# A planned attention and state-space kernel: the prologue laid out anew

## The chip, the cores and the metric

The kernel runs on one core of one Trainium2 chip. The engines named below are TensorE (PE, with its weight loads as PEld), VectorE (DVE), ScalarE (ACT), GpSimd (POOL) and SyncE (SP, which here only issues transfers). The metric is the device time of one execution in microseconds (us). The kernel before takes 701.06 us, the median of three runs between 700.88 and 701.33.

## What is computed

Two results on 2,048 rows of 640 columns stand side by side in the output. The first is a state-space layer on `A_x`, the second is attention with 32 query heads of 20 columns that share one key head and one value head, on `B_x`:

```python
h = Lam_bar[None, :] * h + Bu[:, t, :]              # A: a scan over t, 640 complex states
y = 2.0 * einsum("blp,dp->bld", hseq, Cmat).real + x * Dskip
q = (x @ wq) -> 32 heads of 20; k = x @ wk; v = x @ wv     # B
p = softmax(q k^T * 20 ** -0.5); o = p @ v; out_B = o @ wo
```

Inputs and output are bf16. The attention needs 32 x 2,048 x 2,048 exponentials, 134 million, and this is most of the work.

## The kernel before, in words

**Tiles.** The scores are made as 2,048 blocks of 128 keys x 512 queries. Of a block's 512 queries all belong to one head. Keys and queries have 20 columns plus a row that carries a bound, so a block uses a 32-row strip of the PE array, and three or four blocks run side by side in one *fill* (a matmul in four 32-row strips). A fill goes into a slot of three banks of PSUM, SC0 or SC1. Two or three of its blocks get their exp on ACT (one ACTIVATE over 1,024 or 1,536 columns, line 1519, into PR); the third block of a fill with two is turned by DVE into an approximate exponential (line 864: a scaled conversion to int16, whose bits are read as bf16), to which POOL (line 1834) and DVE add constants for four shifted variants whose products with differently scaled values (VS) are added up. The products with the values (PR with VP, BIG with VS, line 727) run on PE in four 32-column strips and collect in the bank MB3. The last free bank, MB2, and the third banks of the slots serve all the other work: query projections, the state-space part, the output projection.

**The bound.** In place of a maximum over scores, each query's row gets a bound: the absolute query times a matrix that holds the largest absolute key of each column, times a negative constant. `mab` holds the key maxima, `mask0` the constant in the shape of the matrix, M0 their product. M0 times the absolute queries is added to the queries' own PSUM bank; the result, lifted by a constant, is evicted to QT.

**The prologue** does this, in front of the first exp: x of the first two blocks of 512 rows (tb 0 and 1) is loaded as it is (`xn`, into the buffer CT) and turned by PE against a unit matrix, with evictions by ACT and DVE into xbT (lines 1132 and 1135); x of blocks 2 and 3 (`XB`) comes by transposing transfers. Keys of the four blocks are made on PE (line 1155) from wks, four copies of wk beside each other (line 1040, on ACT). After each block's keys DVE takes the maximum over its columns (line 1161) and DVE or ACT evicts the keys to KT (lines 864 and 1167). The first queries (`qt_task`, g = 0) come from wqp (line 1272), are evicted by ACT (line 1285), and wait for M0. DVE takes the maximum of the five partial maxima (line 1187) and makes M0 (line 863). PE adds the product, DVE evicts to QT (line 864), the first fill follows. The last block's keys are made in halves (`KEY_STEPS`), with a reduction for each. Values (`v_task`, line 1211) are made for the blocks 0 and 1 in banks of SC1 in between. Meanwhile the vectors of the state-space part (`vrow`: log_dt, Lambda_re, Lambda_im, Dskip) feed a chain of small steps for its tables.

**The queues.** SP issues Lambda_re, the two plain x loads, Dskip, the first 80 columns of wq, the transposing loads of x, wv, the rest of wq, then the B matrices. ACT's queue issues log_dt, Lambda_im and wk. POOL makes masks, the integer steps of the angle tables, wqp, and fills VS and QT with zeros.

**What sets the order.** The program is not written in the order in which it runs. `Schedule` plays the whole kernel through with durations given for each step: each engine takes, whenever it is free, the ready step of the lowest `prio`, subject to gates (`gate`), to slack that keeps urgent steps free, and to parameters that change with the number of blocks done (`STAGES`). Transfers of the prologue have assumed landing times (`LANDS` and the last column of `XB`). A seed (`SEEDS`) varies it. The order that results is emitted engine by engine, with semaphore waits. So a changed step in the prologue, or another seed, gives another order of everything behind it too.

```python
fill = self.pe([], self.mmt(512, 2), deps=deps, prio=0, mode="S", hook=lambda op, i=i: self.fill(op, i))
```

This is a fill in `attention()`: its deps are the last exps of the slot, the queries of its block, and the keys.

Of the kernel before, what the change touches and what calls it, by code (L numbers as in the profile page):

```python
# [11 lines left out]
ACT = mybir.ActivationFunctionType  # L12
# [454 lines left out]
class Build:  # L467
# [77 lines left out]
    SEEDS, REPLAYS = (10005,), 12  # L545
# [418 lines left out]
    def constants(self):  # L964
# [12 lines left out]
        def fill(t, v, dur):  # L977
            return "dve", lambda e: e.memset(t, v), dur
# [31 lines left out]
        many("VS", [("pool", lambda e: e.memset(p.VS[:], 0.0), 1850)] + [fill(p.VS[:, k, :, 20:21], c, 100) for k, (_, c) in enumerate(self.SHIFTS)])  # L1010
# [12 lines left out]
    def loads(self):  # L1023
# [7 lines left out]
                                       eng=eng, writes=[f"vrow{i}"], prio=0) for i, v in enumerate((self.log_dt, self.Lre, self.Lim, self.Dskip))]  # L1031
        self.vec_op = [vec[0]("act"), vec[1]("sp"), vec[2]("act")]
# [15 lines left out]
        self.vec_op.append(vec[3]("sp"))  # L1048
# [72 lines left out]
    def kv_steps(self):  # L1121
# [20 lines left out]
        def kv(tb):  # L1142
            yield lambda: all((tb, c) in self.xb_op for c in range(NC)) and (tb < self.PLAIN or self.s.done([self.xb_op[tb, 0]])) \
                and any(x in self.early for x in self.free_banks)
            bank = self.take(self.early, self.KEY_BANKS)
            prev = None
            steps = [(0, c, 512) for c in range(NC)] if tb < 3 else self.KEY_STEPS
            for x, c, n in steps:
                at = 512 * tb + n * x
# [4 lines left out]
                else:  # L1154
# [3 lines left out]
                                   self.mmt(n), prio=self.KP[tb], deps=[self.xb_op[tb, c], self.wks_op] + bank.last, prev=prev,  # L1158
                                   mode="F", load=float(n), reads=[f"xbT{tb}_{c}", "wks"], writes=[bank.key])
                if c == NC - 1:  # L1160
                    red = self.dve(lambda e, src=bank.cols(n * x, n * x + n), to=p.mab[:, tb + x:tb + x + 1]: e.tensor_reduce(  # L1161
                        out=to, in_=src, axis=AX.X, op=ALU.max, apply_absolute_value=True), 115 + 1.05 * n, deps=[prev], reads=[bank.key],
                        writes=[f"mab{tb + x}"], prio=0.31 if tb < 3 or x else 0.315)
                    self.red_op[tb + x] = red
            dst, src = p.KT[:, 512 * tb:512 * tb + 512], bank.ap
            if self.KEYS[tb] == "a":
                kt = self.act(lambda e: e.activation(dst, src, ACT.Identity, bias=p.lift[:, 2:3], scale=ALPHA * UNIT), 600,
                              deps=[red, self.lift_op], reads=[bank.key, "lift"], writes=[f"KT{tb}"], prio=0.34)
            else:
                kt = self.dve(self.ts(dst, src, ALPHA * UNIT, p.lift[:, 2:3], ALU.mult, ALU.add), 640,  # L1170
                              deps=[red, self.lift_op], reads=[bank.key, "lift"], writes=[f"KT{tb}"], prio=0.44)
# [4 lines left out]
            if tb < 2:  # L1176
                yield lambda: any(x in self.early for x in self.free_banks)
                yield from self.v_task(tb, self.take(self.early, self.KEY_BANKS))
            else:
                self.tasks.append((self.V_AT[tb - 2], 0, lambda: self.started, lambda bank: self.v_task(tb, bank)))  # L1180
                self.tasks.sort(key=lambda t: t[0])

        self.red_op = {}

        def bound():
            yield lambda: len(self.red_op) == 5
            m = self.dve(lambda e: e.tensor_reduce(out=p.mab[:, 5:6], in_=p.mab[:, 0:5], axis=AX.X, op=ALU.max), 120,
                         deps=list(self.red_op.values()), reads=[f"mab{i}" for i in range(5)], writes=["mabs"], prio=0.3)
# [1427 lines left out]
```

## Time and profile before

| | |
|---|---|
| median of three runs | 701.06 us |
| the profiled execution | 701.27 us, with a span of 699.5 us |
| busy in the span | PE 684.9, ACT 685.4, DVE 630.2, POOL 467.7 us |
| exps on ACT | 677, of which 566 of two blocks and 111 of three |
| granted PE clock | 0.999 of full |

The span runs from the first instruction of the program to the last; the device time has some 1.8 us more around it. In rows of groups, the columns are line, engine, operation, what is written and read (the buffers' numbers are left out, so SC is SC0 or SC1, M is M0), shapes, count; then busy time in us, the mean duration of one in ns; then the idle time of the engine in front of them and what ended it. In rows in order of time the first two numbers are start and duration in us, and what stands in brackets is the idle time ahead and its releaser. A PE row such as `32*128 32x512` is a weight of 32 x 128 against 512 columns. In rows of stretches there is the length, the busy time with the count, the granted clock, the share of the transfer engines and GB/s. Consecutive instructions of an engine overlap a little, so the mean duration of one is longer than its share of the busy time.

### The profile page before, as it was taken

To read this page: it belongs to the slowest core of one execution; us is meant where nothing else is said; L and a number is where in the kernel's file an instruction comes from. 1 tells how busy PE (TensorE), PEld (TensorE's weight loads), DVE (VectorE), ACT (ScalarE), POOL (GpSimd) and SP (SyncE) were. 2 spreads that over 40 slices of the span, in tenths; PEclk is the share of its full clock that TensorE was granted. 3 is DMA by queue.
4 is the path that set the end of the run, shared out by engine and by line. 5 is a ranking of instruction groups with operands and counts; after the bars stand their busy time and mean duration, and the time that the engine had idled before them with its cause. 6 is when DMAs were issued, how large, how long until landed. Compare 5 with 4: busy or idle time off the path is not lost.

```text
span 699.5 us, 27013 instructions
## 1 busy us (share of the span) xinstructions
PE 684.9 (98%) x11350; PEld 248.1 (35%) x11350; DVE 630.2 (90%) x1211; ACT 685.4 (98%) x701; POOL 467.7 (67%) x796
## 2 busy tenths in 40 slices
PE   9999999999999999999999999999999999999997
PEld 5323232334323333534343323334333333343323
DVE  7899899999999988898979997899999999997695
ACT  7999999999999999999999999999999999999996
POOL 4266776443868898464777885767866777768780
PEclk9999999999999999999999999999999999999999
DMA  9649831101111111000030010120000011100101
GB/s 220 174 107 211 184 89 58 28 8 31 28 48 32 28 43 37 22 19 16 17 83 20 15 42 21 36 55 22 12 15 20 12 26 39 32 20 15 27 15 40
DMA packets 77590, 34.46 MB, mean 49 GB/s; under 512 B 58350, under 2 KB 77470, under 8 KB 77470
## 3 DMA queue, kind: packets, MB, share of 16 engines
q1 hardware_dynamic: 76506, 32.44, 19.3%
q8 instruction: 91, 1.49, 0.9%
q10 hardware_dynamic: 964, 0.29, 0.2%
q14 instruction: 29, 0.24, 0.1%
HBM read 11.53 MB, written 9.75 MB: 30 GB/s over the span
## 4 chain that ended last, share of the span: by engine, by line
PE 66%; ACT 33%; DVE 0%; issue 0%; DVEq 0%
ACT PR L1519 33%; PE MB L727 26%; PE MB L797 17%; PE SC L727 14%; PE MB L807 7%; PE SC L1155 1%; PE MB L723 1%; PE SC L723 0%; DVE PR L859 0%; PE MB L1272 0%; DVE mab L1161 0%; DVEq L510 0%; PE SC L1211 0%; DVE pvsb L859 0%; DVE M L863 0%
## 5 line engine op out<-in xcount | busy, mean ns | idle before, releaser
L1519 ACT ACTIVATE PR<-SC 128x1024 bf16<-128x1024 f32 (+1 forms) x677 | 670.5, 1177 | 4.0 <-PE SC L727 2.9
L1834 POOL INT64_ADD BIG<-BIG x761 | 455.4, 614 | 200.8 <-DVE BIG L864 71.8
L864 DVE TENSOR_SCALAR BIG<-SC 128x512 int16<-128x512 f32 x548 | 369.1, 684 | 48.9 <-PE SC L727 42.6
L727 PE MATMUL SC<-QT,KT 32*128 32x512 bf16 x2013 | 264.5, 384 | 7.0 <-ACT PR L1519 6.0
L727 PE MATMUL MB<-BIG,VS 128*32 128x512 bf16 x2332 | 257.4, 383 | 0.4 <-DVE pvsb L1901 0.2
L727 PE MATMUL MB<-PR,VP 128*32 128x512 bf16 x1465 | 213.7, 384 | 0.0
L727 PEld LDWEIGHTS SC<-QT,KT 32*128 32x128 bf16 x2013 | 66.6, 91 | 157.4 <-ACT PR L1519 94.5
L727 PEld LDWEIGHTS MB<-BIG,VS 128*32 128x32 bf16 x2332 | 61.6, 95 | 65.1 <-issue 40.2
L727 PEld LDWEIGHTS MB<-PR,VP 128*32 128x32 bf16 x1465 | 51.4, 94 | 44.6 <-issue 32.5
L797 PE MATMUL MB<-CT,W 128*32 128x320 bf16 (+2 forms) x996 | 52.6, 301 | 0.6 <-issue 0.6
L864 DVE TENSOR_SCALAR BIG<-BIG 128x1024 int16<-128x1024 int16 (+1 forms) x116 | 45.8, 427 | 1.7 <-PE MB L727 1.3
L807 PE MATMUL MB<-xaT,BT 32*128 32x256 bf16 x200 | 38.6, 272 | 0.7 <-ACT PR L1519 0.6
L797 PE MATMUL MB<-CA,W 128*32 128x512 bf16 (+1 forms) x640 | 35.5, 302 | 0.0
L797 PE MATMUL MB<-xaT,BA 128*32 128x256 bf16 x800 | 32.2, 275 | 0.0
L807 PE MATMUL MB<-diagD,xaT 32*128 32x128 bf16 x320 | 31.4, 217 | 0.0
L807 PEld LDWEIGHTS MB<-diagD,xaT 32*128 32x128 bf16 x320 | 17.7, 92 | 28.9 <-ACT PR L1519 19.3
L797 PEld LDWEIGHTS MB<-CT,W 128*32 128x32 bf16 x996 | 22.4, 96 | 15.2 <-issue 7.5
L2086 DVE CAST stg<-MB 128x512 bf16<-128x512 f32 x35 | 23.9, 682 | 2.5 <-PE MB L797 2.5
L797 PE MATMUL MB<-xaT,BT 128*32 128x256 bf16 x600 | 25.1, 274 | 0.0
L859 DVE TENSOR_TENSOR prod<-MB,tab 128x1024 bf16<-128x1024 f32 x20 | 24.3, 1217 | 0.4 <-PE MB L797 0.2
L864 DVE TENSOR_SCALAR BIG<-MB 128x512 int16<-128x512 f32 x35 | 23.8, 679 | 0.0
L2353 DVE TENSOR_TENSOR_SCAN g<-sc,hst,prod 128x256 bf16<-128x256 f32 x30 | 22.9, 774 | 0.1
(174 smaller groups left out, 488.3 us busy)
## 6 DMA issues: line engine op xcount, KB each, us to landing
out_dram<-stg SPq DMA_DIRECT2D x31, 128.0 KB, 1.8
qd<-BIG SPq DMA_DIRECT2D x20, 128.0 KB, 2.4
QT<-qd SPq DMA_DIRECT2D x28, 80.0 KB
OP<-pvsb SPq DMA_DIRECT2D x105, 20.0 KB
rdP<-recs SPq DMA_DIRECT2D x105, 20.0 KB
lbd<-BA SPq DMA_DIRECT2D x5, 320.0 KB, 4.0
CT<-in_B_x_dram SPq DMA_DIRECT2D x2, 640.0 KB, 5.3
BA<-in_A_B_re_dram SPq DMA_DIRECT2D x1, 800.0 KB, 7.0
```

The costliest lines, as they stand in the source:

```text
L723: r = e.matmul(out[32 * j:32 * j + 32], lhsT=lhsT[:, 32 * j:32 * j + 32], rhs=rhs, start=start, stop=stop, tile_position=(0, 32 * j), skip ...
L727: return lambda e: e.matmul(out, lhsT=lhsT, rhs=rhs, start=start, stop=stop, **kw)
L797: x = e.matmul(out[32 * j:32 * j + 32], lhsT=lhsT[:, 32 * j:32 * j + 32], rhs=rhs, start=start, stop=r.end is tag, tile_position=(0, 32 * ...
L807: return lambda e: e.matmul(out, lhsT=lhsT[at], rhs=rhs[at], start=False, stop=r.end is tag, tile_position=(32 * row, 0), skip_group_check ...
L859: return lambda e: e.tensor_tensor(out, a, b, op)
L864: return lambda e: e.tensor_scalar(out, a, s1, s2, op0=op0, op1=op1)
L1155: prev = self.pe([lambda e, x=x, c=c, n=n, at=at: e.matmul(bank.cols(n * x, n * x + n), lhsT=p.wks[:, 128 * c:128 * c + 128], rhs=p.xbT[:, ...
L1519: ex = self.act(lambda e: e.activation(dst, t[:, 0:512 * n], ACT.Exp, scale=1.0 / UNIT), 0.8333 * 512 * n + 64, table="exp", deps=[op], re ...
L1834: op.fns.append(lambda e: e.int64_add(words(dst), words(src), add))
L2086: ev = self.dve(lambda e: e.tensor_copy(st, bank.ap), 645, deps=[prev], reads=[bank.key], writes=[key], prio=self.EV, gate=(lambda: last.e ...
L2353: o = self.dve(lambda e, ri=ri, init=init: e.tensor_tensor_scan(p.g[:, u, ri, :], rdec, p.prod[:, 1, 0, ri, :], init, ALU.mult, ALU.add), ...
```

## The change

The diff does these things.

1. **Queues.** Lambda_re and Dskip move from SP's queue to ACT's, so SP begins with the x loads. The transposing loads of the last x block are cut into pieces of 2, 2 and 1 columns of 128 instead of 3 and 2. The assumed landing times change.
2. **wks** is made by DVE, not ACT (`WKE`); the four small fills of VS go from DVE to POOL.
3. **Keys.** Each block has its own bank (`KEY_BANKS`), the last block is made whole and not in halves; its eviction and that of the third block go to DVE and ACT at later times (`KEYS`, gates).
4. **The bound in steps.** M0 is made from the maximum over three blocks by ACT (line 1188 of the new program), and when the fourth block's maximum is there DVE takes the smaller of that and mask0 times the fourth maximum (line 1192; the constant is negative). The maximum over all four, for the later blocks' bound, follows behind.
5. **First queries in two banks.** The first query block stands half in MB2 and half in a bank of SC1; ACT and DVE evict a half each, before and after the product with M0.
6. **Values** of blocks 0 and 1 are made together, in the free half of MB2, ahead of the product with M0.
7. **The first exp** waits for the first slot's two banks and the keys of the first block, and not for all banks and all keys.
8. **The plan**: another seed, other parameters in some stages, `LAST` 8 instead of 16, `CB_FROM` 341.944 instead of 358.689. With it the whole order is another one: 561 exps of two blocks and 116 of three.

```diff
-    SEEDS, REPLAYS = (10005,), 12
+    SEEDS, REPLAYS = (120680,), 12
...
-        self.vec_op = [vec[0]("act"), vec[1]("sp"), vec[2]("act")]
+        self.vec_op = [vec[0]("act"), vec[1]("act"), vec[2]("act")]
...
-        self.vec_op.append(vec[3]("sp"))
+        self.vec_op.append(vec[3]("act"))
...
-    PLAIN, KP, QR, FRP, SINP, SKIP_P, KEY_BANKS = 2, (1.04, 1.04, 1.06, 1.08), 1.05, 0.34, 0.32, 1.03, "2543016"
-    WKP, QUAD_KEYS, WKE = 0.9, 0, "a"
-    TURNED, KEYS = ("adada", "adada"), "adaa"
-    XB = ((2, 0, 5, 11250.0), (3, 0, 3, 12500.0), (3, 3, 5, 13400.0))
-    LANDS = (2250.0, 2400.0, 2750.0, 8200.0, 5600.0, 7900.0, 6500.0, 8450.0, 14600.0, 17000.0)
+    PLAIN, KP, QR, FRP, SINP, SKIP_P, KEY_BANKS = 2, (1.04, 1.04, 1.06, 1.0), 1.05, 0.34, 0.32, 1.03, ("5", "01", "3", "2")
+    WKP, QUAD_KEYS, WKE = 0.1, 0, "d"
+    TURNED, KEYS = ("adada", "adada"), "adad"
+    XB = ((2, 0, 5, 10850.0), (3, 0, 2, 12050.0), (3, 2, 4, 13270.0), (3, 4, 5, 13900.0))
+    LANDS = (2250.0, 2500.0, 2750.0, 7800.0, 5200.0, 7450.0, 6300.0, 7900.0, 14400.0, 16700.0)
...
         def bound():
-            yield lambda: len(self.red_op) == 5
-            m = self.dve(lambda e: e.tensor_reduce(out=p.mab[:, 5:6], in_=p.mab[:, 0:5], axis=AX.X, op=ALU.max), 120,
...
-            self.m0_op = self.dve(self.ts(p.M0[:], p.mask0[:], p.mab[:, 5:6], None, ALU.mult), 200, port=True,
...
+            yield lambda: all(i in self.red_op for i in range(3))
+            m = self.dve(lambda e: e.tensor_reduce(out=p.mab[:, 4:5], in_=p.mab[:, 0:3], axis=AX.X, op=ALU.max), 120,
...
+            self.m0a_op = m = self.act(lambda e: e.activation(p.M0[:].rearrange("p a b -> p (a b)"), p.mask0[:].rearrange("p a b -> p (a b)"), ACT.Copy,
+                                                scale=p.mab[:, 4:5]), 220,
...
+            yield lambda: 3 in self.red_op
+            self.m0_op = self.dve(lambda e: e.scalar_tensor_tensor(out=p.M0[:], in0=p.mask0[:], scalar=p.mab[:, 3:4], in1=p.M0[:],
+                                                                   op0=ALU.mult, op1=ALU.min), 250, port=True,
...
-    KEY_STEPS = ((0, 0, 512), (0, 1, 512), (0, 2, 512), (0, 3, 256), (0, 4, 256), (1, 3, 256), (1, 4, 256))
...
+        halves = [(bank, 0, 512, key)] if g else [(bank, 0, 256, key), (more, 256, 512, key + "b")]
...
+        if g == 0:
+            yield from self.v_task((0, 1), bank, 256, evs)
         yield lambda: self.m0_op is not None
...
-        mine = [b for _, bs in self.slots for b in bs]
-        yield lambda: all(not b.busy for b in mine)
+        yield lambda: all(not b.busy for b in self.slots[0][1][:-1])
...
-            deps += [self.kt_op[tb] for tb in range(4)]
+            deps += [self.kt_op[tb] for tb in range(min(4, (self.tile_n + 12) // 16 + 1))]
...
-    LAST = 16
+    LAST = 8
...
-    CB_FROM, CB_STEP = 358.689, 15.665
+    CB_FROM, CB_STEP = 341.944, 15.665
```

More of the change, by code (lines that the diff above doesn't have):

```diff
@@ L1405, in attention @@
             i = k % len(self.slots)
+            if k == i and k:
+                bs = self.slots[i][1][:-1]
+                yield lambda: all(not b.busy for b in bs)
+                self.slot_last[i] = [op for b in bs for op in b.last]
             yield lambda: (fill is None or fill.start is not None) and all(o.start is not None
```

178 lines of the change are left out of this document (109 added, 69 removed).

## The prediction

> **What bounds the kernel now.** I read the page first (busy time, chain), then the groups of ACT by form, then the busy time of ACT by stretch, then the first 19 us in order of time. From the page of the kernel before:
>
> ```profile
> span 699.5 us, 27013 instructions
> ...
> PE 684.9 (98%) x11350; PEld 248.1 (35%) x11350; DVE 630.2 (90%) x1211; ACT 685.4 (98%) x701; POOL 467.7 (67%) x796
> ...
> PE 66%; ACT 33%; DVE 0%; issue 0%; DVEq 0%
> ...
> L1519 ACT ACTIVATE PR<-SC 128x1024 bf16<-128x1024 f32 (+1 forms) x677 | 670.5, 1177 | 4.0 <-PE SC L727 2.9
> ```
>
> PE and ACT are both 98% busy, and the chain changes between them. The last row tells which paces: the 677 exps occupy ACT for 670.5 us, and ACT is idle only 4.0 us in front of them. So the time is three pieces: the prologue up to the first exp, the exps nearly back to back, and the tail. The groups of ACT by form, whole span, and then the same view for two neighbouring stretches of 39 us (536:575 and 575:614):
>
> ```profile
> L1519 ACT ACTIVATE PR<-SC 128x1024 bf16<-128x1024 f32 x566 | 532.9, 1106 | 4.0 <-PE SC L727 2.9 <-PE MB L727 0.7
> L1519 ACT ACTIVATE PR<-SC 128x1536 bf16<-128x1536 f32 x111 | 160.2, 1538 | 0.0
> ...
> L1519 ACT ACTIVATE PR<-SC 128x1024 bf16<-128x1024 f32 x38 | 35.9, 1076 | 0.2
> L1519 ACT ACTIVATE PR<-SC 128x1536 bf16<-128x1536 f32 x4 | 6.0, 1502 | 0.0
> ...
> L1519 ACT ACTIVATE PR<-SC 128x1024 bf16<-128x1024 f32 x38 | 36.0, 1081 | 0.9 <-PE SC L727 0.6 <-PE MB L727 0.2
> L1519 ACT ACTIVATE PR<-SC 128x1536 bf16<-128x1536 f32 x3 | 4.5, 1503 | 0.0
> ```
>
> A third block in an exp costs 1538 - 1106 = 432 ns. The stretch from 575 does one such exp fewer in the same 39 us. Busy time of the exps by stretch:
>
> ```profile
> 500.00:575.00 75.00, 74.64 (x78) 1.00 0.07 18
> 575.00:654.00 79.00, 77.47 (x82) 1.00 0.11 27
> ```
>
> ACT misses 0.36 us of 75 and then 1.53 us of 79: from 575 to 654 PE is late with its fills, elsewhere hardly. That is the one place behind the prologue where something is to be had. The prologue in order of time, one view for each engine: SP, ACT, PE's loads and PE, DVE:
>
> ```profile
> 0.81 0.39 SPq L708 DMA_DIRECT2D vrow<-in_A_Lambda_re_dram  x1
> 1.26 0.97 SPq L708 DMA_DIRECT2D CT<-in_B_x_dram  x2
> 2.27 0.49 SPq L708 DMA_DIRECT2D vrow<-in_A_Dskip_dram  x1
> ```
>
> ```profile
> 7.30 0.73 ACT L1040 ACTIVATE wks<-wkr 128x640 bf16<-128x640 bf16 x1
> ...
> 14.88 1.82 ACT L1167 ACTIVATE KT<-SC,lift 128x512 bf16<-128x512 f32 x3
> 18.16 1.02 ACT L1519 ACTIVATE PR<-SC 128x1024 bf16<-128x1024 f32 x1 [1.45 <-PE SC L727]
> ```
>
> ```profile
> 14.36 0.34 PEld L1155 LDWEIGHTS SC<-BIG,wks 128*128 128x128 bf16 x4 [0.31 <-DMA BIG<-in_B_x_dram]
> ...
> 15.05 0.66 PE L1211 MATMUL SC<-wvr,BIG 128*128 128x20 bf16 x20
> 15.57 0.59 PE L727 MATMUL MB<-PR 128*128 128x512 bf16 x2
> 16.35 0.40 PE L727 MATMUL MB<-BIG,M 128*32 128x512 bf16 x4 [0.19 <-DVE M L863]
> ...
> 17.73 0.48 PE L727 MATMUL SC<-QT,KT 32*128 32x512 bf16 x4
> ```
>
> ```profile
> 13.94 0.69 DVE L1161 TENSOR_REDUCE mab<-SC 128x1 f32<-128x512 f32 x1
> 14.55 0.28 DVE L863 TENSOR_SCALAR BIG<-QT 128x512 int16<-128x512 int16 x1
> 15.03 0.76 DVE L1161 TENSOR_REDUCE mab<-SC 128x1 f32<-128x256 f32 x2 [0.19 <-PE SC L1155]
> 15.82 0.16 DVE L1187 TENSOR_REDUCE mab<-mab 128x1 f32<-128x5 f32 x1
> 16.01 0.29 DVE L863 TENSOR_SCALAR M<-mask,mab 128x128 bf16<-128x128 f32 x1
> 16.81 0.81 DVE L864 TENSOR_SCALAR QT<-MB,lift 128x512 bf16<-128x512 f32 x1 [0.51 <-PE MB L727]
> ```
>
> The chain behind the last piece of x is to be seen: PE waits for the transfer until 14.36, two half reductions (to 15.79), their maximum, the bound's matrix M0 (to 16.30), its product with the queries (to 16.75), the last eviction of QT (to 17.62), the first fill, and the exp at 18.16. The exp idles 1.45 us for it.
>
> **The change, part by part.**
>
> *x first in its queue.* The x loads begin at 0.81 where Lambda_re stood, 0.45 us earlier; Dskip (0.49 us) no longer stands between x and the transposes. I take 0.45 for everything that lands behind them: the last piece of x at 13.9 instead of 14.36, wvr at 14.6 instead of 15.05. The transposes of the last block are cut 2, 2, 1 instead of 3, 2, so only one matmul is left behind the last landing. The three vector loads and the load of wk now stand one behind the other on ACT, whose queue grows by two issues (0.39 + 0.49) ahead of its first table load. I count nothing, since ACT's first work waits for a column that DVE makes from these very vectors; without that cover it would be those 0.9 us at most. The Trainium skill ("DMA: Bandwidth & Descriptors", Issuing engines are not separate DMA queues) says that loads of different issuing engines interleave on the same 16 engines, so that only issue time is saved. By that rule the gain is the 0.45 us of issue and no bandwidth; no row here separates the two.
>
> *wks on DVE instead of ACT.* ACT loses 0.73 us, DVE gets a copy of 640 columns between its table steps and its evictions of x. Nearest rows: 0.28 us for 512 16-bit columns on DVE, 0.73 us for this very copy on ACT. I take 0.35, as DVE's own row is nearer in kind; at 0.73 DVE's evictions, and all that hangs on them, come 0.4 us later. The Trainium skill ("VectorE: DVE Perf Modes", What auto-detection actually checks) gives a 16-bit copy within SBUF four elements a cycle, from which I estimate 0.33 us; a copy that missed the mode would take 0.82 by it, and the first exp would come 0.4 to 0.5 us later. The 0.28 us row agrees with the fast mode.
>
> *Maximum in steps, queries in two banks.* Behind the last landing: one matmul to 14.3, one reduction over 512 columns (0.69) to 15.05, one step on M0 (0.29 to 0.35) to 15.4. The maximum over the first three blocks and M0's first form (on ACT) now lie ahead of it, beside the wait for x. But PE now has all 40 value matmuls of blocks 0 and 1 queued in front of the product with M0, behind the landing of wvr: 20 hold PE from 15.05 to 15.57, so 40 take 1.05, from 14.6 to 15.65. So the product starts at 15.65, not 15.45. It is 0.40 as before (two halves of the columns), to 16.05. The eviction is split: DVE takes half the columns, 0.81 - 0.31 = 0.50 (a reduction of half the columns is 0.76 / 2 = 0.38, 0.31 below the whole one), and ACT takes the other half beside it (below the 0.6 that a KT eviction of 512 columns takes). With 0.06 from product to eviction as before, to 16.6; fill and exp follow as before (17.62 to 18.16, 0.54): first exp at 17.15. Gain 1.0 us. Ends: 1.5 if PE's queue is not late and the vectors' removal gives more; 0.45 if DVE is 0.4 late and wvr lands late. On ACT the two KT evictions (0.6 each) stand ahead of the half of QT; they start once the three-block maximum is there (about 14.4) and end at 15.7, 0.3 ahead of their successor's input; later than that by more they would set the first exp.
>
> *First exp waits for fewer keys.* It needs block 0's keys only; the third and fourth evictions go to DVE or behind. Third-bank matmuls of the next query task now wait for KT of block 3 on DVE, one eviction behind the first QT: PE has two exps at 532.9 / 566 = 0.94 us until the third needs its fill. Cost nothing, 0.3 at most.
>
> *The order that is planned anew.* It is the larger part: 561 exps of two blocks and 116 of three, so ACT gets 5 blocks more, at 0.432: +2.16 us. DVE makes 5 conversions fewer and some 24 double additions fewer, POOL 18 more; with DVE at 90% and POOL at 67% I count nothing for that. On PE the number of fills stays 677, and the streams differ by some 7 passes of 512 columns of 2,400, with five changes of mode more: nothing. But they stand elsewhere. Between exps 561 and 640, the stretch 575:654, PE has about 271 passes instead of 284, with as many three-block exps (7): 13 at 0.59 - 0.40 = 0.2 us each (two passes against one in PE's rows) are 2.6 us of room. What ACT lost there is the 1.53 idle plus some slower exps: the stretch did one exp of three blocks fewer than its neighbour in 39 us (1.4 us) and lost 0.6 idle more in its second half; I take 2.1 off. Ends: 0 (the stall moves) and 3. The remaining idle of ACT behind the first exp is 4.0 - 1.45 - 1.53 = 1.0; I halve it, -0.5, since PE gets fewer passes in the tight stretches. Behind the last exp four passes of PE stand instead of one: three at 0.2 are 0.6 at most, nothing where they run beside it; I take +0.1.
>
> Sum: -1.0 + 2.16 - 2.1 - 0.5 + 0.1 = -1.34 us: a span of 698.2. The profiled run took 701.27 us, 1.77 more than its span and 0.21 more than the median of 701.06; so 699.7 us as a median. About 0.2% (1.4 us) is what a measurement of this kernel can tell from no change, and the sum lies just at it.
>
> **Rivals.**
>
> *PE paces.* 66% of the chain speaks for it. Then the five blocks on ACT cost nothing, since ACT only fills its own gaps, and the loosened stretch and the earlier start count in full: -1.0 - 2.1 - 0.1 = about -3: 698.0. Against it: ACT idles only 4.0 us.
>
> *The prologue doesn't get faster.* PE runs in order, and wvr's landing, wk's and wq's stand closer to the work that wants them; DVE has wks in addition. If they eat the 1.0 us, the rest stays: 700.7.
>
> *Slower.* ACT paces, pays 2.16 for its blocks, and the late fills are not gone but moved: the new order was never run under these DMA times, and a stretch like 575:614 (1.3) comes up somewhere in addition. -1.0 + 2.16 + 1.3 + 0.1 = +2.56: 703.6. It decides from 0.2 us more idle than today, where the sum reaches +1.4. For it: nearly every stretch has ACT within half a per cent of full, so each added block shows. Against it: the stretch that is late today has measurably fewer passes.
>
> **How the numbers follow.** Forecast 0.50 at 699.7, its own range 698.8 to 700.6 by the prologue's ends, half of it on either side of -0.2%; PE paces 0.19 (faster); prologue not faster 0.13 (same); slower 0.18. So faster 0.24 + 0.19 = 0.43, same 0.26 + 0.13 = 0.39, slower 0.18. The range takes in the rivals' times but the outer half of each: 697.8 to 702.9.
>
> **What would show it.** The first x load at 0.81, PE's last wait for x ending near 13.9, the value matmuls running up to the product with M0, the first exp at 17.2 (a start above 17.7 says that DVE or wvr was late). The groups of ACT: 116 exps of 1536 at 1.5 us, idle ahead of the exps down from 4.0 to about 2, none of it as dense as 1.53 in 79 us. The prediction is wrong if that idle grows, if the exps take other than 2 us more in all, or if the piece behind the last exp changes by over half a us.

## The result, and the profile after

The changed kernel takes 706.19 us, the median of eight runs between 703.50 and 708.68; the kernel before, run between them, 701.29 (700.88 to 703.32). The ratio is 1.0064, with a 95% interval of 1.0042 to 1.0086: slower, where 699.7 was forecast. The profiled execution of the changed kernel is its quickest one: 703.50 us, with a span of 701.7. From its page, its groups of ACT by form, and the busy time of ACT in the two stretches shown of before and one further ahead:

```profile
span 701.7 us, 26947 instructions
...
PE 683.8 (97%) x11300; PEld 246.9 (35%) x11300; DVE 618.5 (88%) x1178; ACT 685.8 (98%) x701; POOL 478.0 (68%) x818
...
PE 52%; ACT 45%; DVE 2%; DMA 1%; issue 0%; ACTq 0%; DVEq 0%
```

```profile
L1566 ACT ACTIVATE PR<-SC 128x1024 bf16<-128x1024 f32 x561 | 528.2, 1115 | 2.0 <-PE SC L727 1.4 <-PE MB L727 0.2
L1566 ACT ACTIVATE PR<-SC 128x1536 bf16<-128x1536 f32 x116 | 168.2, 1546 | 0.5 <-PE MB L727 0.4
```

```profile
500.00:575.00 75.00, 74.86 (x78) 1.00 0.06 15
575.00:654.00 79.00, 78.50 (x83) 1.00 0.11 30
450.00:500.00 50.00, 49.06 (x52) 1.00 0.20 36
```

Much of what was forecast behind the prologue came: 116 exps of three blocks, idle time ahead of the exps down from 4.0 to 2.5 us, and the stretch from 575 misses 0.50 us instead of 1.53. Most of what was won there stands elsewhere now: between 450 and 500 ACT misses 0.94 us, where the kernel before misses 0.19. DMA has entered the chain with 1%. The start shows why; PE in order of time, first of the kernel before, then of the changed one:

```profile
4.11 0.19 PE L727 MATMUL MB<-ident,vrow 15*128 15x15 bf16 x1
4.23 2.31 PE L727 MATMUL MB<-PR 128*128 128x256 f32 x7
6.38 1.28 PE L727 MATMUL SC<-ident,CT 128*128 128x128 bf16 x20
```

```profile
6.15 0.18 PE L727 MATMUL MB<-ident,vrow 15*128 15x15 bf16 x1 [1.97 <-DMA vrow<-in_A_Lambda_im_dram]
6.25 1.56 PE L727 MATMUL MB<-PR 128*128 128x256 f32 x6
7.65 1.28 PE L727 MATMUL SC<-ident,CT 128*128 128x128 bf16 x20
...
14.28 2.32 PE L1155 MATMUL SC<-BIG,wks 128*128 128x512 bf16 x10
16.43 1.16 PE L1218 MATMUL MB<-wvr,BIG 128*128 128x20 bf16 x40
17.84 0.29 PE L727 MATMUL MB<-BIG,M 128*32 128x256 bf16 x4 [0.24 <-DVE M L1192]
...
18.99 0.40 PE L727 MATMUL SC<-QT,KT 32*128 32x512 bf16 x4
```

The small product of the vectors (MB from ident and vrow) had not waited for a transfer before. Now it waits 1.97 us for Lambda_im. Behind it, in PE's order, stand filler matmuls (MB from PR, which only keep PE busy) and the turning of x (SC from ident and CT). So x, which lands 0.5 us earlier than before (5.13 instead of 5.60, by the trace's landing of the first load), is turned 1.3 us later, and the first exp starts at 19.41 instead of 18.16. The queue of ACT, and the piece of the chain that follows from it:

```profile
0.81 0.57 ACTq L708 DMA_DIRECT2D vrow<-in_A_log_dt_dram  x1
1.42 0.27 ACTq L708 DMA_DIRECT2D vrow<-in_A_Lambda_re_dram  x1
1.72 0.32 ACTq L708 DMA_DIRECT2D vrow<-in_A_Lambda_im_dram  x1
2.08 0.41 ACTq L707 DMA_DIRECT2D wkr<-in_B_wk_dram  x1
2.52 1.02 ACTq L708 DMA_DIRECT2D vrow<-in_A_Dskip_dram  x1
```

```profile
1.72 4.38 DMA vrow<-in_A_Lambda_im_dram
```

1.2 KB are 4.38 us under way. Ahead of them two loads of x of 640 KB each were issued on the other queue, at 0.81 and 1.32. In the kernel before Lambda_im was issued at 1.40, just behind x's first load at 1.26, and was there at 2.71. The runs below test whether this place in time is the cause.

The time between the two profiled runs, in four pieces read from the exps in order of time (the 41st exp is a point behind which the prologue no longer shows):

| | before | changed | difference |
|---|---|---|---|
| first exp starts | 18.16 | 19.41 | +1.26 |
| from there to the 41st exp | 37.62 | 38.33 | +0.71 |
| 41st exp to the end of the last | 635.45 | 634.97 | -0.48 |
| behind the last exp | 8.30 | 8.94 | +0.64 |

That is +2.1 of span. The median is 2.7 above that profiled run; the runs below show where a part of that arises.

### The profile page after: what moved, and what is told of

It is laid out like the page before. It is cut to its first block, busy times and chain, and to the rows that moved or that the text cites. A ratio compares the mean times of both kernels' runs of the same rounds, so it can differ in the third digit from the quotient of the medians.

```text
span 701.7 us, 26947 instructions
## 1 busy us (share of the span) xinstructions
PE 683.8 (97%) x11300; PEld 246.9 (35%) x11300; DVE 618.5 (88%) x1178; ACT 685.8 (98%) x701; POOL 478.0 (68%) x818
## 4 chain that ended last, share of the span: by engine, by line
PE 52%; ACT 45%; DVE 2%; DMA 1%; issue 0%; ACTq 0%; DVEq 0%
ACT PR L1566 44%; PE MB L727 20%; PE MB L797 13%; PE SC L727 10%; PE MB L807 7%; DVE BIG L864 1%; PE SC L1155 1%; DMA vrow<-in_A_Lambda_im_dram 1%; PE MB L723 1%; PE SC L723 0%; DVE PR L859 0%; ACT L2199 0%; DVE pvsb L1950 0%; ACTq L708 0%; DVE mab L1161 0%
## 5 line engine op out<-in xcount | busy, mean ns | idle before, releaser
L1566 ACT ACTIVATE PR<-SC 128x1024 bf16<-128x1024 f32 (+1 forms) x677 | 671.5, 1189 | 2.5 <-PE SC L727 1.4
L1883 POOL INT64_ADD BIG<-BIG x779 | 465.0, 613 | 191.8 <-DVE BIG L864 68.9
L864 DVE TENSOR_SCALAR BIG<-SC 128x512 int16<-128x512 f32 x541 | 364.5, 684 | 62.1 <-PE SC L727 55.8
L727 PE MATMUL MB<-BIG,VS 128*32 128x512 bf16 x2312 | 265.4, 383 | 0.7 <-POOL BIG L1883 0.3
L727 PE MATMUL MB<-PR,VP 128*32 128x512 bf16 x1470 | 221.7, 384 | 0.2 <-ACT PR L1566 0.2
L727 PEld LDWEIGHTS MB<-BIG,VS 128*32 128x32 bf16 x2312 | 64.5, 95 | 65.6 <-issue 38.0
L727 PEld LDWEIGHTS MB<-PR,VP 128*32 128x32 bf16 x1470 | 53.7, 94 | 44.4 <-issue 30.2
L864 DVE TENSOR_SCALAR BIG<-BIG 128x1024 int16<-128x1024 int16 (+1 forms) x90 | 34.3, 422 | 2.4 <-PE MB L727 1.3
L807 PE MATMUL MB<-xaT,BT 32*128 32x256 bf16 x168 | 32.5, 272 | 0.3 <-ACT PR L1566 0.2
L807 PEld LDWEIGHTS MB<-diagD,xaT 32*128 32x128 bf16 x320 | 17.7, 92 | 29.0 <-ACT PR L1566 19.5
L797 PE MATMUL MB<-BIG 128*32 128x512 bf16 x332 | 25.8, 383 | 0.0
```

Source lines behind the costliest of these rows:

```text
L727: return lambda e: e.matmul(out, lhsT=lhsT, rhs=rhs, start=start, stop=stop, **kw)
L797: x = e.matmul(out[32 * j:32 * j + 32], lhsT=lhsT[:, 32 * j:32 * j + 32], rhs=rhs, start=start, stop=r.end is tag, tile_position=(0, 32 * ...
L807: return lambda e: e.matmul(out, lhsT=lhsT[at], rhs=rhs[at], start=False, stop=r.end is tag, tile_position=(32 * row, 0), skip_group_check ...
L864: return lambda e: e.tensor_scalar(out, a, s1, s2, op0=op0, op1=op1)
L1566: ex = self.act(lambda e: e.activation(dst, t[:, 0:512 * n], ACT.Exp, scale=1.0 / UNIT), 0.8333 * 512 * n + 64, table="exp", deps=[op], re ...
L1883: op.fns.append(lambda e: e.int64_add(words(dst), words(src), add))
```

## The experiments

All of them keep the planned order of a kernel and change single places in it afterwards, so that nothing else moves. `put` takes a step out of the planned list, gives it an engine and puts it ahead of or behind another; vec1 is Lambda_re, vec3 Dskip, xn0 the first load of x. The readings of all runs, in us; "before" is the kernel before in the same comparison:

| run | median | before | first exp | 41st exp | 41st to last | behind |
|---|---|---|---|---|---|---|
| after_again | 705.44 | 702.26 | 20.78 | 59.49 | 635.82 | 8.94 |
| lre_on_sp | 704.51 | 702.26 | 18.38 | 58.24 | 635.69 | 8.95 |
| before_vec_on_act | 705.59 | 702.26 | 21.47 | 59.10 | 635.17 | 8.29 |
| dskip_on_sp | 706.60 | 702.26 | 19.34 | 57.96 | 635.48 | 8.95 |
| lre_two_pieces | 703.48 | 701.68 | 17.84 | 57.33 | 635.68 | 8.95 |
| lre_two_pieces_early_max | 703.71 | 701.68 | 18.06 | 57.47 | 635.51 | 8.95 |
| warm_first | 704.62 | 701.68 | 19.50 | 58.69 | 635.52 | 8.95 |
| log_dt_last (a single run) | 703.88 | 701.68 | 19.38 | 57.71 | 635.37 | 8.95 |
| two_pieces_bound_first | 707.91 | 701.45 | 18.26 | 61.31 | 635.57 | 8.94 |
| ten_blocks_fewer | 702.66 | 701.45 | 18.16 | 57.17 | 634.28 | 8.93 |
| before_dskip_on_act | 701.95 | 701.45 | 18.22 | 56.05 | 636.85 | 8.29 |
| before_bound_first | 705.90 | 701.45 | 18.17 | 60.48 | 635.37 | 8.30 |
| two_pieces_again | 704.03 | 701.79 | 18.28 | 57.65 | 635.12 | 8.95 |
| twenty_passes_fewer | 704.37 | 701.79 | 17.97 | 57.66 | 635.37 | 8.93 |
| blocks_and_passes_fewer | 701.70 | 701.79 | 18.18 | 58.42 | 632.62 | 8.95 |
| two_pieces_late_mm | 702.92 | 701.61 | 18.20 | 57.02 | 634.70 | 8.96 |

**Where the vectors stand.** The changed kernel again; Lambda_re alone back on SP; the kernel before with only the vectors moved; Dskip alone back:

```diff
+    put("vec1", "sp", ahead="xn0")        # lre_on_sp, in the changed kernel
+    put("vec1", "act", behind="vec0")     # before_vec_on_act, in the kernel before
+    put("vec3", "act", behind="wk")
+    put("vec3", "sp", behind="xn1")       # dskip_on_sp, in the changed kernel
```

> The changed kernel as it is, once more, so that its scatter and a second profile stand beside the runs below. Theory V (the vectors Lambda_re and Lambda_im, issued on ACT's queue beside the flood of x, land late; PE waits in order for them, and the whole prologue with it): PE's first product with vrow starts at 6 us or later, the first exp at 19.4 or later, 705 to 707 us as a median, with 3 to 5 us between the runs. Theory P (the new order behind the prologue is the slower one, and scatters): the same time, but the first product with vrow may stand anywhere.

> The changed kernel with Lambda_re alone back on SP ahead of x; every other instruction and its order are as in the changed kernel. Theory V: all three vectors land by 2.8 us, PE's product with vrow starts at 4.1, the first exp at 17.2 to 17.7 (2 us sooner), the span is near 699.7, the median 701.5 +- 0.7, and the scatter between runs is under 1.5 us. Theory P: 704.5 us or more, with 3 us or more between the runs, whatever the first exp does.

> The kernel before with nothing but Lambda_re and Dskip moved to ACT's queue (x first on SP); its order behind the prologue is untouched. Theory V: PE waits for vrow until 6 us or later, the first exp comes at 19.3 to 20.2 instead of 18.16, the median is 702.5 to 705, with more scatter than the kernel before. Theory P: the kernel before's time, 701.1 +- 0.7, since its order is the old one.

> The changed kernel with Dskip alone back on SP, behind the two plain loads of x. Theory V: no change, 705 to 707, with PE's wait for vrow as it was, since the first steps need Lambda and log_dt, not Dskip. Rival within V (the sixth issue on ACT's queue, not the place of Lambda, is what delays ACT): 1 to 2 us faster. Theory P: 705 to 707 too.

PE's product with the vectors, in order of time, in before_vec_on_act and then in lre_on_sp:

```profile
6.26 0.17 PE L727 MATMUL MB<-ident,vrow 15*128 15x15 bf16 x1 [2.08 <-DMA vrow<-in_A_Lambda_im_dram]
```

```profile
4.12 0.19 PE L727 MATMUL MB<-ident,vrow 15*128 15x15 bf16 x1
```

The changed kernel repeats itself: PE's product at 6.14, the first exp at 20.78, 705.44 us; its runs lie within 1.7 us, closer than the 3 to 5 that both theories had from the first eight. Two loads of 1.2 KB on another queue, and nothing else, cost the kernel before 3.3 us in its first exp and 3.3 in its median (705.59 against 702.26). That is theory V, shown in the old order: the new one is not needed for the loss. Not all of the 3.3 us is the wait itself, though: PE's product stands 2.15 us later than in the kernel before, and in this profile the fillers behind it run slowly besides (seven in 3.35 us, where they took 2.31; see the scatter below). The band for the first exp (19.3 to 20.2) was too narrow, and 705.59 is above its 705. Dskip's place makes no difference that stands out from the scatter (704.25 to 708.75 in four runs), as expected. lre_on_sp has no wait, and its runs lie within 1.2 us; but its first exp comes at 18.38, not at 17.2 to 17.7, and 704.51 is what theory P wanted (with runs 3 us apart, which they are not). So V is right for the vectors, and is not the whole: in the new order Lambda_re's place is worth 0.93 us of the median (705.44 to 704.51).

**The third transposing load.** In lre_on_sp the last piece of x lands at 15.12, later than the kernel before had it. The step merged back:

```diff
+    piece("xb30", 0, 3)                   # columns of 128: 3 and 2, not 2, 2, 1
+    piece("xb32", 3, 5)
+    order.remove(by["xb34"])
```

> The changed kernel with Lambda_re on SP ahead of x, as in the run before, and the last block of x again turned by two transposing loads (3 and 2 columns of 128) instead of three (2, 2, 1). Theory I (each transposing load holds SP's queue for about 1.3 us however narrow it is, so the third one cost more than the two matmuls it saved): the last landing goes from 15.12 to 14.3 +- 0.2, the first exp from 18.38 to 17.5 +- 0.2, the median from 704.5 to 703.2 +- 0.5. Rival (bytes set the landing, not pieces): last landing still near 14.9 to 15.1, first exp 18.4 to 18.6 as one matmul more stands behind it, 704.5 or a little more.

From the chain of lre_on_sp, then of lre_two_pieces: the holds of SP's queue by the transposing loads, and the last of them on its way to landing:

```profile
2.92 5.61 SPq L712
8.58 1.29 SPq L712
9.91 1.30 SPq L712
11.25 3.87 DMA BIG<-in_B_x_dram
```

```profile
8.60 1.46 SPq L2680
...
10.11 4.27 DMA BIG<-in_B_x_dram
```

A load of 2 columns holds the queue for 1.30 us, one of 3 for 1.46; in lre_two_pieces the one of 2 columns holds it for 1.52. So the price is mostly one per load, and hardly one per column. With two loads the last one lands at 14.38 instead of 15.12, and the first exp comes 0.54 earlier in this profile. Theory I holds for the landing. The first exp, at 17.84, misses the band of 17.3 to 17.7 by a little: two matmuls stand behind the landing again, and PE's 40 value matmuls end just ahead of the product. The median of 703.48 is in its band too, but held against the kernel before of the same comparison it is a gain of only 0.45 (1.80 above it instead of 2.25), and in the repeat below (two_pieces_again, 2.24 above) none. So a gain in the time is not clear of the noise: the earlier landing hardly reaches it.

**The wait filled.** Does the place of the fillers behind the wait matter, or the vectors' own steps on DVE and ACT? And is it Lambda, or the place in time?

```diff
+    for op in warm:                       # warm_first: fillers between vrow's product and x's turning
+        order.remove(op)
+        order.insert(order.index(vrow), op)
+    put("vec0", "act", behind="vec2")     # log_dt_last
```

> The changed kernel with its queues as they are (the vectors land at 6.1), but the PE's two filler matmuls of 256 and two of 512 columns that stood behind the product with vrow now stand ahead of it, so that PE fills the wait with them. Theory W (the wait costs twice: PE idles 2 us, and then runs the fillers, at half speed in some executions because of the idle time, before it turns x): the first turning matmul starts at 6.3 to 6.6 instead of 7.6 to 9.0, the first exp comes at 18.7 to 19.1, the median is 704.3 +- 0.7 and the runs lie within 1.5 us. Rival (the vectors' own chain on DVE and ACT is what is late): first exp at 19.4 or later, 705.5 +- 0.7.

> The changed kernel with log_dt issued third on ACT's queue, behind Lambda_re and Lambda_im. Theory V (the place in time against x's loads decides, not the vector): Lambda_re, now first, lands by 2.4, Lambda_im, second, near 5.2, log_dt, third, near 6.1, and PE's product with vrow starts at 6.1 to 6.3 as before. Rival (something about the Lambdas, such as their place in memory): they land at 5.2 and 6.1 in any place, log_dt by 3.

PE in warm_first:

```profile
6.24 0.18 PE L727 MATMUL MB<-ident,vrow 15*128 15x15 bf16 x1
6.35 1.29 PE L727 MATMUL SC<-ident,CT 128*128 128x128 bf16 x20
7.48 0.38 PE L727 MATMUL MB<-PR 128*128 128x512 bf16 x1
9.56 0.38 PE L1155 MATMUL SC<-BIG,wks 128*128 128x512 bf16 x1 [1.70 <-ACT BIG L1135]
```

PE does turn x at 6.35, and then stands 1.70 us for ACT's first eviction, which is queued on ACT behind the vectors' steps and a table load until 8.83. The first exp is at 19.50: the rival is right about it, although the median came out in theory W's band (with 2.7 us between the runs, not 1.5). In-order waits on three engines lie one behind another here, and removing one uncovers the next. In log_dt_last Lambda_re, now first, lands at 2.25, Lambda_im, second, at 5.22, and log_dt, third, at 5.99, as theory V has it; the place in time decides:

```profile
6.13 0.16 PE L727 MATMUL MB<-ident,vrow 15*128 15x15 bf16 x1 [1.95 <-DMA vrow<-in_A_log_dt_dram]
```

**What is given back within the first 40 exps.** With vectors and transposing loads put right the first exp is 0.3 us ahead of the kernel before, but the 41st is 1.55 behind. Part of it is planned, some 0.85 us: the new order has four exps of three blocks among the first 40, the old one two. The rest is idle time ahead of the 17th and the 19th exp (exps 15 and 17 in the recorded texts). The chain leads there from the tiny transfer mrep (640 values of 4 bytes, from which the later queries' bound is made) over its way back (mcol) and DVE's Mm to the eviction of the next queries. First mrep's start was moved, then its place ahead of the bulk loads, in both kernels, and at last DVE's wait itself:

```diff
+    order.insert(... , late)              # early_max: maximum over four blocks directly behind M0
+    put("bn0", "sp", behind="mo")         # bound_first: B_re and B_im behind mrep
+    put("bn1", "sp", behind="bn0")
+    order.insert(order.index(behind) + 1, mm)   # late_mm: Mm nine DVE instructions later
```

> The same as the run with two pieces, and the maximum over all four blocks' keys, which the round trip for the later queries' bound starts from, is taken on DVE ahead of the first queries' eviction instead of behind it. Theory M (what the earlier first exp gained is given back at exps 15 to 17, because the tiny round trip lands late and DVE's work in order behind it holds the next queries): the round trip is issued at about 16.3 instead of 17.1, its second half lands 0.5 to 0.9 sooner, the loss in the first 40 exps falls from 2.0 to under 1.2, 702.4 +- 0.6. Rival (the round trip ends with the bulk loads that it is queued behind, whenever it was issued): the loss in the first 40 exps as without this edit, and the same time.

> The run with two pieces and the early maximum, and in addition the two large loads of the B matrices are issued behind the tiny round trip (mrep) instead of ahead of it. Theory M (what the first exp gains is lost again at exps 15 to 17, because the round trip lands with the bulk that it is queued with, at 27.7, and DVE's work in order behind it holds the next queries): mrep lands near 21, its way back near 23, the loss in the first 40 exps falls from 1.6 to about 0.6, and the median by about 1.0, to 702.6 +- 0.6. Rival (the tables made from the B matrices are what DVE is late with): the loss in the first 40 exps stays or grows, since the B matrices land 1 to 4 us later: 703.7 to 705.

> The kernel before with the two large loads of the B matrices issued behind the tiny round trip (mrep), otherwise as it is. Theory M: mrep lands near 20 instead of 27.2; the kernel before has its exps there with a loss of only 0.65 in the first 40, so this gains 0.2 at most: within 0.5 of the kernel before. Rival (the B matrices, landing later, hold up DVE's tables): slower by 0.5 to 2 us.

> The run with two pieces, and the one DVE instruction that waits for the round trip's way back (Mm) stands nine instructions later in DVE's order, behind the second eviction of the next queries; PE wants Mm only at 36 us. Theory M (DVE stands still 0.83 us at 29.0 for the round trip, and the next queries' eviction behind it makes exps 15 and 17 late): the wait goes, the evictions come 0.8 sooner, the loss in the first 40 exps falls from 1.66 to 0.6 to 1.0, and the median from 703.5 to 704.0 (the base's two medians) to 702.9 +- 0.5. Rival (the evictions wait for PE's products, not for DVE's turn): the loss stays near 1.5 and the median at the base's.

The chain of lre_two_pieces, then of lre_two_pieces_early_max: mrep from issue to landing.

```profile
17.36 10.31 DMA mrep<-mab
```

```profile
16.52 11.27 DMA mrep<-mab
```

Issued 0.84 earlier, it lands 0.12 later: the rival of that run is right, the landing goes with the bulk around it. Ahead of the bulk it was worse, not better: mrep then took 8.0 us (16.73 to 24.76) nearly by itself, and the B matrices, now behind it, landed at 32.09 instead of 26.85. From DVE's waits between 20 and 40 us, first of two_pieces_bound_first, then of lre_two_pieces:

```profile
DVE CA L864 <- DMA BA<-in_A_B_im_dram: 2.9, 1, 2.9
```

```profile
DVE Mm L859 <- DMA mcol<-mrep: 0.8, 1, 0.8
```

The two kernels lost 4.2 to 4.5 us by it. Here theory M was wrong about the remedy, and the rival (DVE wants the B matrices) right in kind, although the loss is larger than it allowed; the order of the loads before is the good one.

With Mm later on DVE the wait of 0.8 goes. The loss in the first 40 exps is their time above 0.903 us for an exp of two blocks and 1.330 for one of three, the usual distance from one start to the next. It falls from 1.66 to 0.98 us, and the median from 703.48 and 704.03 to 702.92 (1.31 above the kernel before, from 1.80 and 2.24; the intervals overlap). This fits theory M, but doesn't show that the wait at Mm is the cause. In two_pieces_again, the same program as lre_two_pieces, Mm doesn't wait at all, and the loss is 1.55 all the same. DVE waits for PE there, ahead of Mm:

```profile
DVE VP L1227 <- PE SC L727: 0.9, 1, 0.9
```

What goes with the loss is how late DVE begins the evictions of the next queries, whichever wait stands ahead of them: 14.06, 13.95 and 13.15 us behind the first exp in lre_two_pieces, two_pieces_again and two_pieces_late_mm, with losses of 1.66, 1.55 and 0.98. In ten_blocks_fewer, which is no different up to there, it is 13.59 and 1.18. So the path through the evictions is borne out; how much of the gain is Mm's place stays open.

**One issue fewer ahead of the transposing loads.** The kernel before, with Dskip alone on ACT:

```diff
+    put("vec3", "act", behind="wk")
```

> The kernel before with Dskip alone moved from SP to ACT's queue, behind wk; Lambda_re stays ahead of x on SP. Theory Q (x's landings hang on the transfers and on the transposing loads' hold of the queue, not on one issue of 0.5 us ahead of them): last landing 14.2 +- 0.2, first exp 18.0 +- 0.2, the median within 0.5 of the kernel before. Rival (each issue on SP ahead of x's transposing loads counts in full, as the prediction had it): last landing 13.85, first exp 17.7, 0.5 us faster.

Last landing 14.39, first exp 18.22, no gain in the median (701.95 against 701.45): theory Q, at the edge of its bands. The first transposing load holds SP until 8.5 whether it starts at 2.90 or at 3.21. (In this profile there are stalls of 1.6 us between 80 and 90 us that the kernel before and its other two versions don't have; they are left unexplained.)

**What paces behind the prologue.** The forecast charged ACT 0.43 us for each block more. Ten exps of three blocks cut to two; 20 PE passes taken out at the same ten places; both:

```diff
+        op.fns = [lambda e: e.activation(dst[:, 0:2], t[:, 0:1024], ACT.Exp, scale=1.0 / UNIT)]
...
+        gone += [o for o in order[at:] if middle(o)][:2]
```

> The run with two pieces, and in ten of the 116 exps of three blocks, spread over the whole kernel, ACT leaves out the third block (its old values stay in PR, so ten blocks of scores have no exp of their own; PE, DVE and POOL do what they did). Theory A (ACT paces, so each block costs its 0.43 us): the median falls by 4.3 +- 0.6, to 699.2. Rival (PE paces much of the time): by 2 us or less, to 701.5 or more.

> The run with Lambda_re on SP and two transposing pieces once more, as the base of the two runs below: 703.5 +- 0.5.

> The run with two pieces, and 20 PE passes of the products with the values left out, two behind each of the ten places at which the run with ten blocks fewer left out a block on ACT (20 x 0.21 = 4.3 us of PE's work; the output lacks these products). Theory B (PE and ACT are both within a fraction of a per cent of full at these places, so that neither alone buys much): the median falls by 0.5 to 2.0. Rival (PE alone paces): by 3.5 to 4.5, to 699.5. Rival (ACT alone paces): by under 0.3.

> Both: the ten blocks left out on ACT and the 20 passes left out on PE, at the same ten places. Theory B: the two together give what neither gives alone, a fall of 3.3 to 4.5 us, to about 699.6, while the parts alone give 0.8 and 0.5 to 2.0. Rival (PE alone paces): the same as the passes alone. Rival (something else, DVE or the transfers, paces): under 2 us for both together.

All ten places lie behind the 41st exp. From there to the end of the last exp the base (lre_two_pieces and two_pieces_again) takes 635.68 and 635.12 us. Against their mean: without the blocks it takes 634.28 (-1.1 of 4.3), without the passes 635.37 (nothing), without both 632.62 (-2.8). These are single profiles, and the two of the base differ by 0.56. In the medians: 702.66, 704.37 and 701.70 against 703.48 and 704.03; above the kernel before 1.21, 2.58 and -0.09 against 1.80 and 2.24. Neither engine alone paces: theory A's 4.3 us for the blocks did not come, and when one engine has less to do it soon waits for the other. One of the ten places, ACT in ten_blocks_fewer in order of time (line 2696 is the shortened exp):

```profile
230.88 1.21 ACT L2696 ACTIVATE PR<-SC 128x1024 bf16<-128x1024 f32 x1
231.92 1.09 ACT L1566 ACTIVATE PR<-SC 128x1024 bf16<-128x1024 f32 x1
233.22 3.77 ACT L1566 ACTIVATE PR<-SC 128x1024 bf16<-128x1024 f32 x4 [0.21 <-PE SC L727]
```

One exp later ACT waits for PE's fill, and the 0.43 is gone: from the shortened exp to the start of the second one behind it are 2.34 us, and 2.33 in lre_two_pieces, where that exp has three blocks. Theory B's mechanism holds, but its sizes were too large: nothing instead of 0.5 to 2.0 for the passes alone, and for both 1.8 to 2.3 in the median and 2.8 in the stretch instead of 3.3 to 4.5. By the medians alone the passes' run is that of "ACT alone paces", but the blocks' run, at a quarter of its price, excludes that. For both together the rival "something else, DVE or the transfers, paces" allowed under 2 us, and the medians lie on either side of that, so a third bound is not excluded. What holds the rest was not tried.

No version came out faster than the kernel before; the best of the new order that does all the work, two_pieces_late_mm, is 1.3 us slower (ratio 1.0018, interval 1.0009 to 1.0027).

## Why the prediction was wrong, point by point

**Where it went.** The profiled pair misses the forecast by 3.5 us: 2.3 up to the first exp (forecast -1.0, measured +1.26), 0.7 from there to the end of the last (-0.44 and +0.23), 0.5 behind it (+0.1 and +0.64). The median adds 2.7.

**The vectors: the step that failed.** "I count nothing, since ACT's first work waits for a column that DVE makes from these very vectors; without that cover it would be those 0.9 us at most." The working counted the issues on ACT's queue and not the landing. The column on which it leaned is itself late when the vectors are. What was missing is the wait for the landing: PE stands 1.97 us for Lambda_im. The bound was wrong too: moving the two loads cost 3.3 us in the old order (with slow fillers in that profile). The sign was in the profile of before and was not used: Dskip, issued 0.6 us behind x's second load, landed at 8.12, 5.8 us later. Of the rivals "PE runs in order, and wvr's landing, wk's and wq's stand closer" comes nearest; it names PE's order, but other loads, and allowed only for the loss of the gain. "Slower" (703.6) had the direction and not the mechanism: it wanted a stall like that of 575 to 614 somewhere in addition, and the idle time ahead of the exps fell.

**x first in its queue.** The 0.45 us came for the plain loads (5.60 to 5.13, 7.88 to 7.19), and not for the last piece (14.88 instead of the forecast 13.9) nor for wvr (15.10 instead of 14.6). The step took the cut into 2, 2 and 1 columns as one matmul gained and priced no load; a further load holds SP's queue for 1.26 to 1.30 us, and undoing it brought the landing 0.74 us forward. Where nothing is cut, x first does give 14.32 to 13.95 (before_vec_on_act).

**wks on DVE.** Taken 0.35, measured 0.48 us; by the Trainium skill ("VectorE: DVE Perf Modes", Side-by-side: where the cycles go for N=2048 bf16) the estimate is 0.33 at four elements a cycle, 0.50 at two and 0.82 at one. The trace lies near that for two, a case that the working left out. It did not decide.

**Maximum in steps, queries in two banks.** Right, and nearly in each term: the step on M0 0.35 (0.29 to 0.35), DVE's half of QT 0.55 (0.50), ACT's 0.47 (below 0.6), the 40 value matmuls 1.16 (1.05). From the last landing to the first exp 3.25 us were forecast; lre_on_sp takes 3.26 (15.12 to 18.38), the kernel before 3.84. This gain of 0.6 is real and is spent on the late landing.

**First exp waits for fewer keys.** Nothing was counted, and the first eight exps run without idle time between them.

**The planned order.** Forecast +2.16 - 2.1 - 0.5 = -0.44 from the first exp to the end of the last; measured +0.2 in the profiled pair (673.30 against 673.08), with the stretch from 575 rid of two thirds of its stall, as said. From the 41st exp on the two orders cost the same in all the runs that do the whole work there and have no stall of their own: 635.2 to 635.5 in the old order, 634.7 to 635.8 in the new. So the sum was 0.7 off, and its terms were not prices: the five blocks more were to add 2.16 us to the exps, and their busy time grew by 1.0 (670.5 to 671.5); leaving out ten blocks gave a quarter of what that step would give for ten. The forecast took ACT as the pace and "PE paces" as a rival; at the places tried neither of the two paces alone. (In the sum of that rival the last term should be +0.1, as in the forecast; its 698.0 goes with that.)

**Behind the last exp.** +0.1 was taken, 0.6 was the end given: +0.64 in every run of the new order. PE's passes behind the last exp do not run beside it; ACT waits for them, in the changed kernel:

```profile
693.86 0.60 ACT L1955 ACTIVATE pvsb<-MB 128x512 bf16<-128x512 f32 x1 [1.15 <-PE MB L727]
```

The kernel before has 0.50 there. The prediction had named a change of over half a us behind the last exp, and exps that take other than 2 us more, as signs of being wrong; both came.

**The scatter.** The profiled run was 2.7 us quicker than the median; the working carried its sum from one profiled execution to the median by a constant, which was right for the kernel before and is not for this one. In after_again, with the same wait for Lambda_im, the first exp comes 1.37 us later. PE there, to be held against the fillers of 6.25 to 7.65 above:

```profile
6.14 0.19 PE L727 MATMUL MB<-ident,vrow 15*128 15x15 bf16 x1 [1.96 <-DMA vrow<-in_A_Lambda_im_dram]
6.26 2.93 PE L727 MATMUL MB<-PR 128*128 128x256 f32 x6
8.98 1.81 PE L727 MATMUL SC<-ident,CT 128*128 128x128 bf16 x20
```

The same six fillers take 2.93 instead of 1.56 us, half the speed, and everything behind them is later by that. With the vectors early the fillers still run at different speeds (1.56 in lre_two_pieces, 2.72 in lre_two_pieces_early_max), but then the landing of the last piece of x, at 14.38 and 14.34, covers it, and the first exps lie 0.2 us apart. So the late vectors also took away the cover that kept most of this lottery out of the time; theory W's "because of the idle time" is not borne out, as it happens without idle time too. In after_again, 2.6 us longer than the profiled run before it, it is 1.37 us; how much of the median's 2.7 it explains, beside small stalls of PE later on, stays open.

## What to carry to other kernels

A small load that an in-order engine waits for early belongs ahead of the bulk in time, on whichever queue; count its landing and not its issue, and look how a like load behind the bulk fared in the profile at hand. Each transposing load has a price of its own, so a finer cut must win more than that. Where two engines are both 98% busy, as here, don't give an edit to one of them the price of its row: take away from both, or measure. And read the same wait in a repeat of the run before calling it a cause: here it was gone in the repeat, and the loss was not.

## What the runs showed of the hardware

- A load of 1.2 KB issued 0.6 to 0.9 us behind 640 KB on another queue takes 3.9 to 4.4 us (Lambda_re lands at 5.29 and Lambda_im at 6.10, one beside the end of x's first load at 5.13); issued 0.14 to 0.18 us behind it, 1.3 us in one run (landed at 2.71) and 2.6 in another (lre_on_sp, 1.43 to 4.07). The Trainium skill ("DMA: Bandwidth & Descriptors", Queues, rings and completion order) has each transfer engine take turns between queues packet by packet. From that I had no reason to expect a wait as long as the whole first load, and that is what the trace shows. It lists single pieces (1,280 bytes of x, 55 ns each in the median; 256 bytes of a vector), but not how many of them an engine takes in one turn, which could reconcile the two.
- A transfer of 640 values of 4 bytes (2.5 KB) takes 8.0 us with no bulk load issued ahead of it but one that landed 1.6 us into it (two_pieces_bound_first), and the 800 KB load issued behind it takes 12.5 us (B_re, issued at 17.10, landed at 29.57), where it takes 7.4 in lre_two_pieces.
- A transposing load of 1 to 3 columns of 128 (512 rows) holds SP's queue for 1.26 to 1.63 us, without a clear price per column.
- PE runs the same six fillers in anything from 1.56 to 2.93 us from one execution to the next. The granted clock in the stretch of 6.2 to 7.6 us is given as 1.00 both for the changed kernel's 1.56 us and for the 2.93 of after_again. The Trainium skill ("TensorE: Matmul & The Clock Gate", Part 1: The HAM clock gate) says that the clock rises after some 3.4 us of sustained work, in a window that runs freely, so that the number of slow matmuls changes from run to run. The trace agrees with the change from run to run, and its clock column does not show it.
